# Routing as single operations behind every sixth product, small two-operand ones on GpSimd

## The chip, the core and the metric

One NeuronCore of a Trainium2 chip runs the kernel. The metric is device time in microseconds for one execution, the median of several; lower is better. The engines of the core work side by side, each through its own queue in order: TensorE (PE in the profile, PEld its weight loads), VectorE (DVE), ScalarE (ACT), GpSimd (POOL) and the queue that issues most DMAs (SP).

## What is computed

A linear attention with a feature map, and behind it a mixture of experts in which every token goes to one expert (top 1 of 8).

```python
def phi(x):
    proj = np.einsum('bhsd,df->bhsf', x, w_phi)
    proj = proj - np.max(np.abs(proj), axis=-1, keepdims=True)
    return np.concatenate([np.exp(proj), np.exp(-proj)], axis=-1)
q_p, k_p = phi(q), phi(k)
kv = np.einsum('bhsf,bhsd->bhfd', k_p, v)
z = np.sum(k_p, axis=2)
attn = np.einsum('bhsf,bhfd->bhsd', q_p, kv) / (np.einsum('bhsf,bhf->bhs', q_p, z)[..., None] + 1e-06)
x = attn.transpose(0, 2, 1, 3).reshape(N, D)        # N = 4608 tokens, D = 512

logits = x @ w_gate                                 # 8 experts
expert_idx = np.argmax(logits, axis=1)
probs = np.exp(logits - logits.max(-1, keepdims=True))
probs /= probs.sum(-1, keepdims=True) + 1e-09
gate_w = probs[np.arange(N), expert_idx]
for e in range(8):
    mask = expert_idx == e
    out[mask] = gate_w[mask, None] * (np.maximum(x[mask] @ w1[e], 0.0) @ w2[e])
```

There are 8 batches, 8 heads, 576 positions and 64 elements per head; the hidden size of an expert is 1024.

## The kernel before

**Attention.** The work is cut into 16 units: 4 groups of two batches (`NG`), and in each group 4 pairs of heads (`NPR`). A unit projects q and k (`project`, L246 to L253): three products into a PSUM tile `ps_proj`, of which there are two, then on VectorE a maximum `mx` (L252) and a difference `t` (L253). The difference ends the use of the PSUM tile, so that TensorE can begin the next projection but one only when `t` is done. ScalarE takes exponentials of `t` (for q after a transpose `pt` on TensorE, L284, which reads `t`). k's exponentials are split into two parts, `kh` on ScalarE and `kl` on GpSimd or VectorE (L275); the raw inputs are split likewise (`xh`, `xl`, L234 and L235) and so is v (`vh`, `vl`, L302 and L303). The products of k with v go to `pk` (L315), one `pk` for each batch. A copy `kvT` by ScalarE (L332) follows each. Four small products `pf` (L341) fold the gate's weights in, and the products `pn` (L363) of q's features give the attention output and the logits, which VectorE normalizes (`rec`, `xrow`, `lgc`).

**Order.** Python emits the unit's work as two lists of items which `merge` interleaves by their weights: the features of this and the next unit on one side, and `first_half` or `second_half`, the products of the previous unit, on the other. `ordered` ties the products into one sequence. The tile framework's scheduler may then move instructions by priority, which normally follows the emission order and which `tc.high_priority` raises. The result is a fixed queue for each engine.

**Routing.** When the four units of a group are through, the group's tokens are routed: `route` (from L571) sums the logits (`lg`), takes the maximum (`lmax`), subtracts it, marks the first expert that reaches it (`cand`, `choice`, `oh_b`), counts tokens of each expert (`gsum`, `base`), and finds each token's rank within its expert by ten bf16 products into `prk` with a triangle of ones. From the ranks come `rkb` (rank divided by 128) and `rkr` (its remainder) and for each of nine token tiles two selection matrices, `sel_p` on VectorE and `sel_h` on GpSimd. The gate value is computed from `ex` and `se` and stored (`gt`). `prk`, `pk` and `pf` share one PSUM pool of two buffers, `ps_kv`, so that the buffer of `prk` is free again only after the product `rks` (L631) has read it. The steps of `route` are a list of functions; `spread` puts one behind every eighth item of the half units of the next group, from its second unit on (u = 5, 9 and 13). For the last group the routing runs by itself, in two parts (`final` is False or True there and None before), between attention and experts. Before the last group's end, `lead` picks the fullest expert from the first three groups, so that its weights can be loaded early.

**Experts.** Tokens are gathered by expert into blocks of 128, 17 pairs of blocks and then single ones, and pass through two products split into three parts each (L936 to L938, L956 to L958).

## Time and profile before

| | |
|---|---|
| median of 3 runs | 953.48 us (951.97 to 954.35) |
| the profiled execution | 955.01 us, of which its span 953.2 us |
| mean granted TensorE clock | 0.968 of full speed |
| PE busy | 909.2 us, 95% |
| VectorE, ScalarE, GpSimd busy | 607.4, 592.6 and 489.3 us |

The span runs from the first to the last instruction. A row of the timeline gives start, duration, engine, line and operation, the tiles written and read, their shapes, how many instructions are merged in the row, and in brackets how long the engine had been idle and what released it. Attention fills the first 440 us or so, the experts the rest.

### The profile page before, as it was taken

The numbers are of one execution on the slowest core, as the hardware profiler recorded it, in microseconds if no ns is written. First come the engines' busy times: TensorE is split into PE (matmuls) and PEld (weight loads), VectorE is DVE, ScalarE is ACT, GpSimd is POOL, SyncE is SP. The second block draws the span as 40 slices with busy tenths as digits, with TensorE's granted clock in tenths as the row PEclk, the third lists the DMA queues.
The fourth block names the chain that finished last, engine by engine and source line by source line (L and its number), as shares of the span: only waits on it lengthen the run. The fifth ranks groups of instructions, "written<-read, shape, count | busy, mean of one in ns | idle before, by whom it ended". The sixth has DMA issues, their size and how long they took to land. (4 is left out here: it accounts for less than half of the span.)

```text
span 953.2 us, 18418 instructions
## 1 busy us (share of the span) xinstructions
PE 909.2 (95%) x6824; PEld 853.8 (90%) x6824; DVE 607.4 (64%) x1046; ACT 592.6 (62%) x895; POOL 489.3 (51%) x325
## 2 busy tenths in 40 slices
PE   6999989999899989999899999999999999999995
PEld 5899989999799989998889999999999999987884
DVE  7767778677987779865854444444444444457850
ACT  5977765777758765762565555555555555568961
POOL 6656666766476667653453333333333333347741
PEclk7999998999999998997999999999999999999998
DMA  4333332333233332143024224341343643764100
GB/s 146 90 103 102 97 100 78 89 107 92 60 103 103 104 102 68 48 147 118 17 95 156 67 91 154 127 150 56 105 155 113 211 154 122 225 219 136 44 23 14
DMA packets 64348, 102.38 MB, mean 107 GB/s; under 512 B 10686, under 2 KB 28478, under 8 KB 64256
## 3 DMA queue, kind: packets, MB, share of 16 engines
q1 hardware_dynamic: 56928, 80.34, 27.3%
q0 software_dynamic: 6720, 20.80, 7.0%
q8 instruction: 54, 0.88, 0.4%
q14 instruction: 38, 0.31, 0.1%
q10 hardware_dynamic: 608, 0.05, 0.0%
HBM read 136.74 MB, written 20.26 MB: 165 GB/s over the span
## 5 line engine op out<-in xcount | busy, mean ns | idle before, releaser
L894 DVE TENSOR_TENSOR wl<-raw,wh 128x1024 fp32r<-128x1024 f32 x137 | 181.2, 1336 | 139.3 <-ACT wh L893 135.4
L893 ACT CAST wh<-raw 128x1024 fp32r<-128x1024 f32 x184 | 191.6, 1050 | 102.7 <-PE po L958 69.2
L894 POOL TENSOR_TENSOR wl<-raw,wh 128x1024 fp32r<-128x1024 f32 x47 | 117.8, 2510 | 176.7 <-ACT wh L893 169.2
L363 PE MATMUL pn<-kf,qp 128*128 128x73 f32 x1024 | 160.9, 261 | 0.0
L363 PEld LDWEIGHTS pn<-kf,qp 128*128 128x128 f32 x1024 | 155.6, 198 | 0.2
L937 PE MATMUL pm<-xl,wh 128*128 128x256 f32 x544 | 154.8, 285 | 0.0
L938 PE MATMUL pm<-xh,wl 128*128 128x256 f32 x544 | 154.7, 284 | 0.0
L936 PE MATMUL pm<-xh,wh 128*128 128x256 f32 x544 | 154.2, 284 | 0.0
L252 DVE TENSOR_REDUCE mx<-ps_proj 128x4 f32<-128x512 f32 (+1 forms) x160 | 100.7, 631 | 70.5 <-PE ps_proj L248 70.2
L275 POOL TENSOR_TENSOR kl<-e,kh 128x1024 fp32r<-128x1024 f32 x47 | 112.9, 2402 | 57.5 <-ACT kh L273 57.5
L235 POOL TENSOR_TENSOR xl<-xr,xh 128x512 fp32r<-128x512 f32 (+2 forms) x62 | 87.0, 1406 | 92.0 <-ACT xh L234 92.0
L246 PE MATMUL ps_proj<-w_hi,xh 128*128 128x256 f32 x288 | 93.8, 326 | 16.8 <-DVE choice L589 10.0
L956 PE MATMUL po<-wh,hh 128*128 128x512 f32 x272 | 109.6, 403 | 0.0
L957 PE MATMUL po<-wl,hh 128*128 128x512 f32 x272 | 107.4, 395 | 0.0
L958 PE MATMUL po<-wh,hl 128*128 128x512 f32 x272 | 106.8, 392 | 0.7 <-DVE hl L944 0.7
L937 PEld LDWEIGHTS pm<-xl,wh 128*128 128x128 f32 x544 | 105.0, 193 | 2.5
L936 PEld LDWEIGHTS pm<-xh,wh 128*128 128x128 f32 x544 | 104.8, 193 | 2.6
L938 PEld LDWEIGHTS pm<-xh,wl 128*128 128x128 f32 x544 | 105.0, 193 | 0.0
L253 DVE TENSOR_TENSOR t<-ps_proj,mx 128x512 f32<-128x512 f32 (+1 forms) x160 | 100.9, 632 | 3.2
L315 PE MATMUL pk<-kh,vl 128*64 128x256 f32 x320 | 99.0, 309 | 2.4 <-POOL vl L303 2.4
L315 PE MATMUL pk<-kl,vh 128*65 128x256 f32 x320 | 99.6, 311 | 1.2 <-POOL kl L275 0.8
L315 PE MATMUL pk<-kh,vh 128*65 128x256 f32 x320 | 99.6, 311 | 0.3 <-DVE vh L302 0.3
(207 smaller groups left out, 2048.8 us busy)
## 6 DMA issues: line engine op xcount, KB each, us to landing
raw<-w SPq DMA_DIRECT2D x184, 512.0 KB
vt<-vv SPq DMA_DIRECT2D x16, 640.0 KB
x_dram<-xrow SPq DMA_DIRECT2D x30, 256.0 KB
xr<-kT SPq DMA_DIRECT2D x15, 320.0 KB
xr<-qT SPq DMA_DIRECT2D x15, 320.0 KB
xr<-kT SPq DMA_DIRECT2D x17, 256.0 KB
xr<-qT SPq DMA_DIRECT2D x17, 256.0 KB
x_dram<-xrow SPq DMA_DIRECT2D x32, 32.0 KB
```

Of the source, the lines that this page charges most:

```text
L253: V.tensor_tensor(t[:, 0 : 2 * n, :], psv, mx[:, 0 : 2 * n].unsqueeze(2).to_broadcast([P, 2 * n, F]), op=ALU.subtract,)
L275: eng.tensor_tensor(kl, e[:, 0:m], kh, op=ALU.subtract)
L315: return T.matmul(st["pk", bb][0:n, hh, :], (vl if j == 1 else vh)[:, 2 * (c + (bb if c == 8 else 0)) + hh, 0:n], (kl if j == 2 else kh)[: ...
L363: m = T.matmul(st["pn"][:, 2 * (c % 3) + hh, :], qp[:, s, s0 + hh, :] if c < 8 else qp[:, s, hh, bb : bb + 2].rearrange("p b q -> p (b q)" ...
L893: A.copy(th, raw[k])
L894: (G if k in (POOL_LO if u else POOL_LO0) else V).tensor_tensor(tl, raw[k], th, op=ALU.subtract)
L936: T.matmul(pm[:, i], th, xh[:, k, :], start=(k == 0), stop=False)
L937: T.matmul(pm[:, i], th, xl[:, k, :], start=False, stop=False)
L938: T.matmul(pm[:, i], tl, xh[:, k, :], start=False, stop=(k == KD - 1))
L956: T.matmul(po, hh[:, i, r], th[:, c], start=(i == j == 0), stop=False)
L957: T.matmul(po, hh[:, i, r], tl[:, c], start=False, stop=False)
L958: T.matmul(po, hl[:, i, r], th[:, c], start=False, stop=(i == 1 and j == 3))
```

## The change

The functions of `route` become one operation each for the three early routings, and `spread` puts one behind every sixth item. The variable `X` stands for VectorE in the last group's routing and for GpSimd in the three others; on `X` run the subtraction of the maximum, the two operations of `cand`, the copies `onehot`, `base_b`, `blk`, `rkr` and `gt`, and the additions to `base` and `se`. Reductions, `oh_b`, the two integer operations on the ranks, the reciprocal and `sel_p` stay on VectorE. The product `rks` is emitted right behind the matmuls of `prk`, for the early routings at a raised priority. For the last group the functions are joined again into steps like those of before. Line numbers of the new code lie up to 34 further down.

```diff
--- before.py
+++ after.py
@@ -458,7 +458,7 @@
         res, k = [], 0
         for i, it in enumerate(items):
             res.append(it)
-            if i >= 8 and i % 8 == 0 and k < len(steps):
+            if i >= 6 and i % 6 == 0 and k < len(steps):
                 res.append((0, steps[k]))
                 k += 1
         del steps[:k]
@@ -574,45 +574,61 @@
         js = slice(j0, j0 + n)
         r = {}
 
-        def choose():
-            lg = sg.tile([P, NC, E], F32, name="lg")[:, 0:n]
+
+
+        X = V if final is not None else G
+
+        def tile_of(name, shape, dtype=F32, **kw):
+            r[name] = sg.tile(shape, dtype, name=name, **kw)[:, 0:n]
+            return r[name]
+
+        def logits():
             V.tensor_reduce(
-                lg, lgc[:, c0 : c0 + n].rearrange("p c h e -> p c e h"), axis=AX.X, op=ALU.add
+                tile_of("lg", [P, NC, E]),
+                lgc[:, c0 : c0 + n].rearrange("p c h e -> p c e h"),
+                axis=AX.X,
+                op=ALU.add,
             )
-            lmax = sg.tile([P, NC], F32, name="lmax")[:, 0:n]
-            V.tensor_reduce(lmax, lg, axis=AX.X, op=ALU.max)
-            V.tensor_tensor(lg, lg, lmax.unsqueeze(2).to_broadcast([P, n, E]), op=ALU.subtract)
-            cand = sg.tile([P, NC, E], F32, name="cand")[:, 0:n]
-            V.tensor_scalar(cand, lg, 0.0, -float(E), op0=ALU.is_ge, op1=ALU.mult)
-            V.tensor_tensor(cand, cand, iota_e.unsqueeze(1).to_broadcast([P, n, E]), op=ALU.add)
-            first = choice[:, js]
-            V.tensor_reduce(first, cand, axis=AX.X, op=ALU.min)
-            oh_b = sg.tile([P, NC, E], BF16, name="oh_b")[:, 0:n]
+
+        def top():
+            V.tensor_reduce(tile_of("lmax", [P, NC]), r["lg"], axis=AX.X, op=ALU.max)
+
+        def shift():
+            X.tensor_tensor(r["lg"], r["lg"], r["lmax"].unsqueeze(2).to_broadcast([P, n, E]), op=ALU.subtract)
+
+        def candidates():
+            cand = tile_of("cand", [P, NC, E])
+            X.tensor_scalar(cand, r["lg"], 0.0, -float(E), op0=ALU.is_ge, op1=ALU.mult)
+            X.tensor_tensor(cand, cand, iota_e.unsqueeze(1).to_broadcast([P, n, E]), op=ALU.add)
+
+        def first_top():
+            V.tensor_reduce(choice[:, js], r["cand"], axis=AX.X, op=ALU.min)
+
+        def one_hot():
+            oh_b = tile_of("oh_b", [P, NC, E], BF16)
             V.tensor_tensor(
                 oh_b,
                 iota_em.unsqueeze(1).to_broadcast([P, n, E]),
-                first.unsqueeze(2).to_broadcast([P, n, E]),
+                choice[:, js].unsqueeze(2).to_broadcast([P, n, E]),
                 op=ALU.is_equal,
             )
-            r["lg"], r["oh_b"] = lg, oh_b
+            X.tensor_copy(onehot[:, js, :], oh_b)
+            r["base_b"] = sg.tile([P, E], BF16, name="base_b")
+            X.tensor_copy(r["base_b"], base)
 
         def count():
-            oh_b = r["oh_b"]
-            oh = onehot[:, js, :]
-            base_b = sg.tile([P, E], BF16, name="base_b")
-            V.tensor_copy(base_b, base)
             if final:
                 pc = ps_kv.tile([P, E], F32, name="pc", tag="pk")
-                T.matmul(pc, ones, base_b, start=True, stop=False)
+                T.matmul(pc, ones, r["base_b"], start=True, stop=False)
                 for c in range(n):
-                    T.matmul(pc, ones, oh_b[:, c, :], start=False, stop=(c == n - 1))
+                    T.matmul(pc, ones, r["oh_b"][:, c, :], start=False, stop=(c == n - 1))
                 place(pc)
-            V.tensor_copy(oh, oh_b)
+
+        def sum_up():
             if not final:
                 gsum = sg.tile([P, E], F32, name="gsum")
-                V.tensor_reduce(gsum, oh.rearrange("p c e -> p e c"), axis=AX.X, op=ALU.add)
-                V.tensor_tensor(base, base, gsum, op=ALU.add)
-            r["base_b"] = base_b
+                V.tensor_reduce(gsum, onehot[:, js, :].rearrange("p c e -> p e c"), axis=AX.X, op=ALU.add)
+                X.tensor_tensor(base, base, gsum, op=ALU.add)
 
         def count_ranks():
             oh_b, base_b = r["oh_b"], r["base_b"]
@@ -624,21 +640,21 @@
                     prk[:, c + 1 :, :], ones, oh_b[:, c : c + 1, :].to_broadcast([P, m, E]), start=False, stop=False
                 )
             T.matmul(prk, ones, base_b.unsqueeze(1).to_broadcast([P, n, E]), start=False, stop=True)
-            r["prk"] = prk
+            with tc.high_priority(offset=200 if final is None else 0):
+                V.tensor_tensor(tile_of("rks", [P, NC, E]), prk, onehot[:, js, :], op=ALU.mult)
 
         def rank():
-            rks = sg.tile([P, NC, E], F32, name="rks")[:, 0:n]
-            V.tensor_tensor(rks, r["prk"], onehot[:, js, :], op=ALU.mult)
-            rki = sg.tile([P, NC], I32, name="rki")[:, 0:n]
             with nc.allow_low_precision("ranks are integers"):
-                V.tensor_reduce(rki, rks, axis=AX.X, op=ALU.add)
-            rkb = sg.tile([P, NC], I32, name="rkb")[:, 0:n]
-            V.tensor_single_scalar(rkb, rki, 7, op=ALU.arith_shift_right)
-            V.tensor_copy(blk[:, js], rkb)
-            V.tensor_single_scalar(rki, rki, P - 1, op=ALU.bitwise_and)
-            rkr = sg.tile([P, NC], F32, name="rkr", bufs=2)[:, 0:n]
-            V.tensor_copy(rkr, rki)
-            r["rkr"] = rkr
+                V.tensor_reduce(tile_of("rki", [P, NC], I32), r["rks"], axis=AX.X, op=ALU.add)
+
+        def rank_parts():
+            rkb = tile_of("rkb", [P, NC], I32)
+            V.tensor_single_scalar(rkb, r["rki"], 7, op=ALU.arith_shift_right)
+            V.tensor_single_scalar(r["rki"], r["rki"], P - 1, op=ALU.bitwise_and)
+
+        def rank_values():
+            X.tensor_copy(blk[:, js], r["rkb"])
+            X.tensor_copy(tile_of("rkr", [P, NC], bufs=2), r["rki"])
 
         def select_a(c):
 
@@ -657,18 +673,36 @@
                 )
 
         def gate():
-            ex = sg.tile([P, NC, E], F32, name="ex")[:, 0:n]
-            A.activation(ex, r["lg"], AF.Exp)
-            se = sg.tile([P, NC], F32, name="se")[:, 0:n]
-            V.tensor_reduce(se, ex, axis=AX.X, op=ALU.add)
-            V.tensor_scalar_add(se, se, 1e-9)
-            V.reciprocal(se, se)
+            A.activation(tile_of("ex", [P, NC, E]), r["lg"], AF.Exp)
+
+        def gate_sum():
+            V.tensor_reduce(tile_of("se", [P, NC]), r["ex"], axis=AX.X, op=ALU.add)
+            X.tensor_scalar_add(r["se"], r["se"], 1e-9)
+
+        def gate_store():
+            V.reciprocal(r["se"], r["se"])
             gt = sg.tile([P, NC, XW - DM], F32, name="gt", bufs=2)
-            V.tensor_copy(gt[:, 0:n], se.unsqueeze(2).to_broadcast([P, n, XW - DM]))
+            X.tensor_copy(gt[:, 0:n], r["se"].unsqueeze(2).to_broadcast([P, n, XW - DM]))
             store_rows(g, gt, DM, XW - DM, c0, n)
 
-        steps = [choose, count, count_ranks, rank] + [lambda c=c: select(c) for c in range(n)] + [gate]
-        return steps if final is not None else [choose] + PAUSE * [pause] + steps[1:3] + PAUSE * [pause] + steps[3:]
+        steps = [logits, top, shift, candidates, first_top, one_hot]
+        selects = [lambda c=c: select(c) for c in range(n)]
+        ranks = [rank, rank_parts, rank_values]
+        gates = [gate, gate_sum, gate_store]
+        if final is not None:
+
+            def all_of(fs):
+                return lambda: run(fs)
+
+            return [
+                all_of(steps),
+                all_of([count, sum_up]),
+                count_ranks,
+                all_of(ranks),
+                *selects,
+                all_of(gates),
+            ]
+        return steps + [sum_up] + PAUSE * [pause] + [count_ranks, pause] + ranks + selects + gates
 
 
     ON_ACT = (0, 2, 4, 6, 8)
```

**VectorE at the beginning of an early routing, before.** `lg` to `oh_b` are the routing's, `mx` and `t` the projections'.

```order
L584 TENSOR_TENSOR lg<-lg,lmax 128x72
L252 TENSOR_REDUCE mx<-ps_proj 128x4
L586 TENSOR_SCALAR cand<-lg 128x72
L663 TENSOR_REDUCE se<-ex 128x9
L587 TENSOR_TENSOR cand<-cand,iota_p 128x72
L253 TENSOR_TENSOR t<-ps_proj,mx 128x512
L589 TENSOR_REDUCE choice<-cand 128x9
L252 TENSOR_REDUCE mx<-ps_proj 128x4
L591 TENSOR_TENSOR oh_b<-iota_em,choice 128x72
L253 TENSOR_TENSOR t<-ps_proj,mx 128x512
```

VectorE at the same place after the change, from `lmax` on:

```order
L594 TENSOR_REDUCE lmax<-lg 128x9
L253 TENSOR_TENSOR t<-ps_proj,mx 128x512
L252 TENSOR_REDUCE mx<-ps_proj 128x4
L605 TENSOR_REDUCE choice<-cand 128x9
L253 TENSOR_TENSOR t<-ps_proj,mx 128x512
L609 TENSOR_TENSOR oh_b<-iota_em,choice 128x72
L252 TENSOR_REDUCE mx<-ps_proj 128x4
L630 TENSOR_REDUCE gsum<-onehot 128x8
L253 TENSOR_TENSOR t<-ps_proj,mx 128x512
```

Three of the routing's operations went to GpSimd, the sum `se` stands further down, and `choice` and `gsum` now stand where a result of GpSimd is waited for, with a `t` behind each.

**GpSimd at the same place after the change.** Before, only `kl` and `xl` stood here.

```order
L275 TENSOR_TENSOR kl<-e,kh 128x1024
L597 TENSOR_TENSOR lg<-lg,lmax 128x72
L601 TENSOR_SCALAR cand<-lg 128x72
L235 TENSOR_TENSOR xl<-xr,xh 128x512
L602 TENSOR_TENSOR cand<-cand,iota_p 128x72
L275 TENSOR_TENSOR kl<-e,kh 128x1024
L615 CAST onehot<-oh_b 128x72
```

The moved operations stand between the splits of k and of the inputs: the second operation of `cand` behind an `xl`, `onehot` behind a `kl`.

**VectorE in the second half of an early routing, before.** `kf` is the copy of the four `pf`.

```order
L351 COPY kf<-pf 128x292
L636 TENSOR_SCALAR rkb<-rki 128x9
L253 TENSOR_TENSOR t<-ps_proj,mx 128x256
L637 CAST blk<-rkb 128x9
L638 TENSOR_SCALAR rki<-rki 128x9
L664 TENSOR_SCALAR se<-se 128x9
L603 CAST base_b<-base 128x8
L640 CAST rkr<-rki 128x9
L665 RECIPROCAL se<-se 128x9
L655 TENSOR_SCALAR sel_p<-iota_pb,rkr,part_133 128x128 x6
```

Between `kf` and the first `sel_p` stand eight operations, of which seven are the routing's. VectorE there after the change, from the `t` behind `kf` on:

```order
L253 TENSOR_TENSOR t<-ps_proj,mx 128x512
L644 TENSOR_TENSOR rks<-prk,onehot 128x72
L648 TENSOR_REDUCE rki<-rks 128x9
L252 TENSOR_REDUCE mx<-ps_proj 128x4
L652 TENSOR_SCALAR rkb<-rki 128x9
L253 TENSOR_TENSOR t<-ps_proj,mx 128x512
L390 TENSOR_SCALAR rec<-pn 128x6
L653 TENSOR_SCALAR rki<-rki 128x9
L391 RECIPROCAL rec<-rec 128x6
L393 TENSOR_TENSOR xrow<-pn,rec 128x384
L399 TENSOR_TENSOR lgc<-pn,rec 128x3x16
L671 TENSOR_SCALAR sel_p<-iota_pb,rkr,part_133 128x128 x9
```

`rks` stands behind the copy `kf` and no longer ahead of it, the casts and the `se` operations are gone, and the nine `sel_p` now stand in one row.

**GpSimd at that second place, after the change.** `blk` and `rkr` were VectorE's before.

```order
L303 TENSOR_TENSOR vl_158<-vt,vh_156 128x1280
L617 CAST base_b<-base 128x8
L656 CAST blk<-rkb 128x9
L235 TENSOR_TENSOR xl<-xr,xh 128x512
L657 CAST rkr<-rki 128x9
L671 TENSOR_SCALAR sel_h<-iota_pb,rkr,hbase 128x128 x4
L275 TENSOR_TENSOR kl<-e,kh 128x1024
L671 TENSOR_SCALAR sel_h<-iota_pb,rkr,hbase 128x128 x5
```

`rkr`, which `sel_p` and `sel_h` read, stands behind a `vl` and an `xl`.

## Rows read from the trace of the kernel before

**Rows 1.** Waits of PE: line waited for and releaser, us in total, times, longest.

```profile
PE ps_proj L246 <- DVE choice L589: 10.0, 3, 3.4
...
PE pf L341 <- DVE rks L631: 3.9, 3, 1.3
PE pp L834 <- DVE bsel L823: 2.5, 1, 2.5
```

**Rows 2.** Timeline of ACT: the copy `kvT` that ends a unit (columns as above).

```profile
129.92 0.58 ACT L332 COPY kvT<-pk 65x512 f32<-65x512 f32 x1 [2.75 <-PE pk L315]
...
164.33 0.58 ACT L332 COPY kvT<-pk 65x512 f32<-65x512 f32 x1 [3.00 <-PE pk L315]
...
188.63 0.58 ACT L332 COPY kvT<-pk 65x512 f32<-65x512 f32 x1 [1.82 <-PE pk L315]
...
237.30 0.58 ACT L332 COPY kvT<-pk 65x512 f32<-65x512 f32 x1 [2.75 <-PE pk L315]
...
270.38 0.58 ACT L332 COPY kvT<-pk 65x512 f32<-65x512 f32 x1 [2.98 <-PE pk L315]
...
343.38 0.58 ACT L332 COPY kvT<-pk 65x512 f32<-65x512 f32 x1 [2.76 <-PE pk L315]
...
376.49 0.58 ACT L332 COPY kvT<-pk 65x512 f32<-65x512 f32 x1 [2.99 <-PE pk L315]
```

**Rows 3.** Timeline of PE at the stops of the first routing and at one of `lead`.

```profile
137.64 0.36 PE L246 MATMUL ps_proj<-w_hi,xh 128*128 128x256 f32 x1
...
142.64 0.55 PE L246 MATMUL ps_proj<-w_hi,xh 128*128 128x256 f32 x1 [3.34 <-DVE choice L589]
...
154.34 0.44 PE L341 MATMUL pf<-fold,kvT 65*128 65x73 f32 x2 [1.29 <-DVE rks L631]
...
403.65 0.39 PE L246 MATMUL ps_proj<-w_hi,xh 128*128 128x256 f32 x1 [1.29 <-DVE t L253]
```

**Rows 4.** Stretches of 5 us: length, busy (x instructions) of PE, PEld, DVE, ACT, POOL; PEclk.

```profile
140.00:145.00 5.00, 2.36 (x12) 2.39 (x13) 4.66 (x9) 2.19 (x3) 1.81 (x2) 0.71 0.21 59
...
405.00:410.00 5.00, 4.84 (x52) 4.84 (x53) 4.65 (x9) 3.03 (x7) 0.40 (x1) 1.00 0.24 69
```

**Rows 5.** Timeline of DVE at the beginning of the first routing.

```profile
136.09 0.21 DVE L583 TENSOR_REDUCE lmax<-lg 128x9 f32<-128x72 f32 x1
...
138.61 1.76 DVE L586 TENSOR_SCALAR cand<-lg 128x72 f32<-128x72 f32 x1
...
140.43 1.47 DVE L587 TENSOR_TENSOR cand<-cand,iota_p 128x72 f32<-128x72 f32 x1
141.82 0.68 DVE L253 TENSOR_TENSOR t<-ps_proj,mx 128x512 f32<-128x512 f32 x1
...
143.15 0.22 DVE L591 TENSOR_TENSOR oh_b<-iota_em,choice 128x72 bf16<-128x72 f32 x1
```

**Rows 6.** Timeline of POOL in the first routing.

```profile
136.71 1.28 POOL L235 TENSOR_TENSOR xl<-xr,xh 128x512 fp32r<-128x512 f32 x1 [6.18 <-ACT xh L234]
137.95 2.37 POOL L275 TENSOR_TENSOR kl<-e,kh 128x1024 fp32r<-128x1024 f32 x1
...
154.97 2.68 POOL L303 TENSOR_TENSOR vl<-vt,vh 128x1280 fp32r<-128x1280 f32 x1
```

**Rows 7.** Groups of POOL instructions by line: count, busy us, mean ns, idle before.

```profile
L154 POOL TENSOR_SCALAR neg_h<-hbase 128x36 f32<-128x36 f32 x1 | 1.1, 1065 | 0.1
...
L844 POOL TENSOR_TENSOR ends<-start,singles 1x8 f32<-1x8 f32 x1 | 0.2, 191 | 1.1 <-DVE start L563 1.1
```

**Rows 8.** Timeline of DVE in the second half of the first routing.

```profile
156.08 1.60 DVE L636 TENSOR_SCALAR rkb<-rki 128x9 int32<-128x9 int32 x1
...
159.25 1.51 DVE L655 TENSOR_SCALAR sel_p<-iota_pb,rkr,part 128x128 bf16<-128x128 bf16 x6
...
165.13 0.42 DVE L252 TENSOR_REDUCE mx<-ps_proj 128x2 f32<-128x256 f32 x1
```

**Rows 9.** Timeline of POOL in a unit without routing.

```profile
195.41 1.30 POOL L235 TENSOR_TENSOR xl<-xr,xh 128x512 fp32r<-128x512 f32 x1 [5.36 <-ACT xh L234]
```

## The prediction

> **What bounds the kernel now.** Read first who makes TensorE wait, since it is busy nearly all the time. Of the waits that fall into attention, the largest is that of a projection for VectorE's `choice`, 10.0 us in 3 times, and another is that of `pf` for `rks`, 3.9 us in 3 times [rows 1]: one of each for each early routing, 13.9 us together.
>
> Then read what a unit takes, from the copy `kvT` at its end to the next one. The unit behind the first routing takes 188.63 - 164.33 = 24.30 us. The three units in which a routing begins take 34.41, 33.08 and 33.11 us [rows 2]. Against 24.30 that is 10.11, 8.78 and 8.81, in all **27.7 us**. So 13.8 us more are lost than the stops show. The reader sees where at the first routing: TensorE stops 3.34 us and 1.29 us [rows 3], and in the slice around the first stop the granted clock is 0.71, a mixture of the full 2.4 GHz and of half of it [rows 4]. I read the 13.8 us as work at the lower level behind six stops, 2.3 us for each (the ranks' own short products are in it). Not every stop is followed by it: the one of 1.29 us at 403.65 [rows 3] has a clock of 1.00 in the slice behind it [rows 4].
>
> Last, why VectorE is late. `cand` has 72 elements in a row of the tile and yet took 1.76 us, its second operation 1.47 us, while `lmax`, which reads as many, took 0.21 us [rows 5]. The 1.76 us end at 140.37, and GpSimd's `kl`, 2.37 us long, ends at 140.32 [rows 6]. Operations on VectorE without a reduction, with all operands in SBUF, stand still here while GpSimd works on a large two-operand one. Behind them stands `t`, 141.82 to 142.50, and TensorE goes on at 142.64.
>
> **The change part by part.**
>
> *The moved operations at the first stop.* Off VectorE's path go the subtraction and both of `cand`. They now run on GpSimd, and `choice` waits for them there. I replay the first routing. `lmax` ends at 136.30 [rows 5]. The price of a small operation on GpSimd does not show in this form; the nearest rows are 0.19 us for 8 elements of two operands and 1.07 us for 36 elements of one [rows 7]. I take 0.3 us, near the lower row, because that one has two operands and waited for nobody, and from the large ones: `kl` takes 2.37 us for 1024 elements, so 72 are 0.17 us plus a start. Then: subtraction to 136.6, first `cand` to 136.9, the `xl` in between (1.28 us [rows 6]) to 138.2, second `cand` to 138.5, `choice` to 138.7, `t` (0.68) to 139.4. TensorE stopped 3.34 us before 142.64, at 139.3. With the handing over it stops about 0.3 us instead of 3.3.
>
> *What is late next.* `oh_b` stays on VectorE behind that `t`, and its operands are all in SBUF. In its row it took 0.22 us [rows 5], but GpSimd was between two of its large operations then. After the change a `kl` starts at 138.5 and holds until 140.9. I take it that `oh_b` waits as `cand` did, to 141.0; `mx` behind it to 141.6; `onehot` on GpSimd meanwhile to 141.3; `gsum` to 141.8; the next `t` to 142.5. TensorE needs that `t` for a transpose. What it has before that is six projection products and four others; the same kind of run went from 137.64 to 139.3 before the stop [rows 3], 1.6 us with the drain. So from 139.6 it works to 141.0 or a little later and then stops 1.5 us. Together the first place costs 1.8 us of stop instead of 3.3.
>
> The Trainium skill, page "SBUF — State Buffer", section "Who interferes with whom", says that a VectorE operation with two SBUF inputs contends with a GpSimd one that reads SBUF, that the loser blocks for the whole instruction, and that a reduction never contends. The trace agrees in the 1.76 and the 0.21 us of [rows 5]; by that rule the stop behind `oh_b` stands, by `oh_b`'s own row of 0.22 us it would not.
>
> *Ranks right behind their matmuls.* `rks` is no longer queued behind other work with the pool's buffer in its hand, and the `prk` products now stand behind the four `pf` of their half unit, not ahead of them. The 1.29 us stop of `pf` goes, three times. What hides the next wait for that buffer is the rest of the half unit's products.
>
> *Ranks to selections.* Before, from the first `sel_p` at 159.25 to the next `mx` at 165.13, VectorE served no projection for 5.9 us and TensorE did not stop [rows 8]: that long its other products cover. In the new order there is no projection served from the `t` behind `rkb` through all nine `sel_p`. Between them: the integer remainder, which may stand still for a `vl` of 2.68 us [rows 6], as `rkb` did for 1.60 us [rows 8], I take 2.2; `rec`, `xrow` and `lgc`, some 0.9; the wait for `rkr`, which GpSimd does behind `blk` and an `xl`, 0.3 + 1.28 + 0.3 less the 0.9 = 1.0; nine `sel_p` at 1.51 / 6 [rows 8] = 2.3. The sum is 6.4, from 4.2 without the `vl` to 6.9 with all of it. Over the cover of 5.9 it is 0 to 1.0, and as TensorE now runs at the full clock there, where cover is used up fastest, I take 1.0, the upper end.
>
> *The rest, at nothing.* The gate's operations moved to GpSimd are not waited for by TensorE; they run in GpSimd's gaps, 5.36 us at once in a unit without routing [rows 9], and would cost their 0.3 us each if the gaps were gone. One step behind six products and not behind eight makes 27 steps fit in one and a half units as 20 did. The last group's routing keeps its operations on VectorE; only their order changes a little ahead of `bsel`, for which TensorE waits 2.5 us [rows 1]; between half a microsecond gained and lost, I take 0. DMA queues get the same transfers; the store of `gt` on SP now waits for GpSimd, with the next input loads behind it, and comes earlier in the routing than before, so I count nothing.
>
> **Sum.** Stops for one routing: 1.8 + 1.0 = 2.8 us instead of 4.6. Of the lower clock: the stop of 1.5 us is longer than all that were followed by it (1.29), that of 1.0 us is shorter, so I count the first always and the second in half of the cases: 4.5 times 2.3 = 10.4 us for three routings. Left of the 27.7 us are 3 x 2.8 + 10.4 = 18.8 us, and the gain is 8.9 us. I take 1 us off, for stops of some tenths that the new handings between engines bring, and forecast a gain of **8 us**. The profiled execution would go from 955.0 (span 953.2) to 947.0. It stands 1.5 us above the median of 953.5; by that the median goes to **945.5 us**.
>
> **Rivals.**
>
> *The waits only change their place.* If the small operations cost what the dearer row says, 1.07 us [rows 7], three of them and `onehot` are 3.1 us later than in the replay; the first stop is then 2.6 us or more, the second as before, all six stops are followed by the lower clock, and 3 x (2.6 + 1.5 + 1.0) + 13.8 = 29 us stand against 27.7: 953.5 to 955, no difference. For it speaks that GpSimd does them in order between operations of 1.28 to 2.68 us. Against it speaks the row of 0.19 us.
>
> The Trainium skill, page "Perfetto Trace Analysis", section "Optimizing Scalar/DVE Operations", warns that moving work from VectorE to GpSimd might not help, because they share a read port; by it this rival is the forecast. The trace shows the sharing, but also that the moved operations pay it now.
>
> *`oh_b` does not wait.* Its only rows are short. Then the stop of 1.5 us is gone, and left are 3 x (0.3 + 1.0) and three times 2.3 us at most, 10.8 us: a gain of 17, 936.5.
>
> *Slower: GpSimd's queue holds up the products.* `gt` on GpSimd waits for VectorE's reciprocal, and other small ones for `lmax`, `oh_b`, `gsum` and `se`; behind each stand the `kl`, `xl` and `vl` that the products of k and v need. It decides when these waits and the ten operations (3 us) together are more than the 5.36 us of idle time [rows 9]. If three of the waits are as long as a `kl`, 7.1 us, 4.7 us come through in each routing, on top of the 2.8, with at least two spells of the lower clock: 3 x (4.7 + 2.8 + 4.6) = 36.3 against 27.7, 8.6 us slower, 962.
>
> **Chances.** Forecast (a gain of 3 to 12 us) 0.60, `oh_b` free 0.14, only a change of place 0.19, held-up products 0.07. A difference of 0.3%, 2.9 us, is about what a measurement can tell from none. Faster by more: 0.74, within: 0.19, slower: 0.07. The range leaves out the slower rival and the better part of the `oh_b` one and reaches into the no-difference case: 939 to 952.5.
>
> **What would show it.** In the new profile: the wait for `choice` at 0.5 us or less in the three places and none of `pf` for `rks` (right); `oh_b` at 1 us or more in the mean, and a transpose `pt` or a projection waiting 1 to 2 us for VectorE just after; a projection waiting some 1 us behind the nine `sel_p`; units of 28 to 32 us in which a routing begins, and perhaps the next one a little long. Wrong would be: `kl` of GpSimd as a new releaser of `pk`, small operations of 1 us on GpSimd, or an `oh_b` of 0.2 us.

## The result and the profile after

The changed kernel takes **942.32 us** (median; 937.23 to 942.77) against 953.06 us beside it: ratio 0.9866, 95% interval 0.9846 to 0.9886. Run a second time, beside the last experiments, it took 938.97 us against 954.45, ratio 0.9845 (0.9821 to 0.9869). By the medians it is faster by 10.7 us in the first comparison and by 15.5 in the second, where 8 were forecast; the ratios on record are not the quotients of these medians, which are 0.9887 and 0.9838. The profiled execution went from 955.0 to 942.1 us. All of its 12.9 us lie in attention: at the first `kvT` of [rows 2] the two traces agree (129.92 and 129.87 us), and the last `kvT` stands at 434.28 us before and at 421.39 after.

Waits of TensorE after the change (line waited for and releaser, us in total, times, longest), to be read against [rows 1]:

```profile
PE pt L284 <- DVE t L253: 9.2, 7, 1.6
...
PE ps_proj L246 <- DVE t L253: 3.1, 5, 0.8
```

No wait of TensorE is put down to `choice` or `rks` any more. In their place stand short ones for `t`, most often of the transposes. The copies `kvT` on ScalarE, which answer [rows 2]:

```profile
129.87 0.58 ACT L332 COPY kvT<-pk 65x512 f32<-65x512 f32 x1 [2.75 <-PE pk L315]
...
158.76 0.58 ACT L332 COPY kvT<-pk 65x512 f32<-65x512 f32 x1 [2.64 <-PE pk L315]
...
183.15 0.58 ACT L332 COPY kvT<-pk 65x512 f32<-65x512 f32 x1 [2.76 <-PE pk L315]
...
231.81 0.58 ACT L332 COPY kvT<-pk 65x512 f32<-65x512 f32 x1 [2.75 <-PE pk L315]
...
262.12 0.58 ACT L332 COPY kvT<-pk 65x512 f32<-65x512 f32 x1 [2.65 <-PE pk L315]
...
335.16 0.58 ACT L332 COPY kvT<-pk 65x512 f32<-65x512 f32 x1 [2.76 <-PE pk L315]
...
364.11 0.58 ACT L332 COPY kvT<-pk 65x512 f32<-65x512 f32 x1 [2.66 <-PE pk L315]
```

The three units with a routing take 28.89, 30.31 and 28.95 us instead of 34.41, 33.08 and 33.11; the unit behind the first takes 24.39. The excess of the three over 24.30 us fell from 27.7 to 15.3 us. TensorE's stops at the first routing [rows 3]:

```profile
139.86 0.36 PE L246 MATMUL ps_proj<-w_hi,xh 128*128 128x256 f32 x1 [0.61 <-DVE t L253]
...
142.82 0.63 PE L284 MATMUL pt<-ident,t 128*128 128x128 f32 x4 [1.43 <-DVE t L253]
...
154.34 0.66 PE L284 MATMUL pt<-ident,t 128*128 128x128 f32 x4 [1.55 <-DVE t L253]
```

Three stops, 3.6 us together, where there were two of 4.6. The second and third routing show the same three within 0.04 us. Stretches of 5 us around stops (length, busy of PE, PEld, DVE, ACT, POOL, then PEclk, DMA share and GB/s), as [rows 4]:

```profile
140.00:145.00 5.00, 3.57 (x32) 3.40 (x33) 5.00 (x8) 3.98 (x8) 4.20 (x5) 1.00 0.16 47
...
245.00:250.00 5.00, 5.00 (x35) 5.00 (x35) 4.45 (x12) 3.26 (x6) 2.31 (x3) 0.72 0.23 54
...
360.00:365.00 5.00, 5.00 (x51) 5.00 (x49) 4.62 (x18) 1.97 (x5) 4.79 (x7) 1.00 0.87 250
```

Between 120 and 395 us the granted clock fell at one place only, around 245 us; behind the other stops it stayed at 1.00. Before, it fell around all three first stops [rows 4] and behind all three second ones, of which the first is:

```profile
155.00:160.00 5.00, 5.00 (x36) 5.00 (x35) 4.64 (x15) 2.66 (x5) 4.57 (x4) 0.66 0.48 128
```

Summing (1 - PEclk) times 5 us over the stretches from 120 to 395 us gives 11.9 us before and 1.7 after. That, and not the stops (13.9 and 10.7 us), is where most of the gain of this pair of profiles lies. There is one profile of the kernel before, and its mean granted clock of 0.968 is at the low end of that kernel's executions (0.968 to 0.984), so its 11.9 us may be more than usual.

VectorE at the two places:

```profile
138.89 0.23 DVE L605 TENSOR_REDUCE choice<-cand 128x9 f32<-128x72 f32 x1 [1.46 <-POOL cand L602]
139.03 0.68 DVE L253 TENSOR_TENSOR t<-ps_proj,mx 128x512 f32<-128x512 f32 x1
139.63 1.66 DVE L609 TENSOR_TENSOR oh_b<-iota_em,choice 128x72 bf16<-128x72 f32 x1
...
142.00 0.67 DVE L253 TENSOR_TENSOR t<-ps_proj,mx 128x512 f32<-128x512 f32 x1
...
151.34 2.35 DVE L652 TENSOR_SCALAR rkb<-rki 128x9 int32<-128x9 int32 x1
153.61 0.68 DVE L253 TENSOR_TENSOR t<-ps_proj,mx 128x512 f32<-128x512 f32 x1
...
155.92 2.30 DVE L671 TENSOR_SCALAR sel_p<-iota_pb,rkr,part 128x128 bf16<-128x128 bf16 x9
```

And GpSimd:

```profile
136.32 0.31 POOL L597 TENSOR_TENSOR lg<-lg,lmax 128x72 f32<-128x72 f32 x1 [5.84 <-DVE lmax L594]
136.72 0.47 POOL L601 TENSOR_SCALAR cand<-lg 128x72 f32<-128x72 f32 x1
137.27 1.29 POOL L235 TENSOR_TENSOR xl<-xr,xh 128x512 fp32r<-128x512 f32 x1
138.51 0.34 POOL L602 TENSOR_TENSOR cand<-cand,iota_p 128x72 f32<-128x72 f32 x1
138.81 2.38 POOL L275 TENSOR_TENSOR kl<-e,kh 128x1024 fp32r<-128x1024 f32 x1
...
150.98 2.68 POOL L303 TENSOR_TENSOR vl<-vt,vh 128x1280 fp32r<-128x1280 f32 x1
...
155.27 0.19 POOL L657 CAST rkr<-rki 128x9 f32<-128x9 int32 x1
```

`oh_b` starts 0.8 us into `kl` and ends 0.1 us behind it; `rkb` starts 0.4 us into `vl` and ends 0.03 us behind it. Each time a `t` that TensorE needs stands behind it in VectorE's queue: at once behind `rkb`, and behind two short operations after `oh_b`.

### The profile page after: what moved, and what is told of

Same layout as the page of the kernel before. It is cut to its first block, busy times and chain, and to the rows that moved or that the text cites. A ratio compares the mean times of both kernels' runs of the same rounds, so it can differ in the third digit from the quotient of the medians.

```text
span 940.1 us, 18395 instructions
## 1 busy us (share of the span) xinstructions
PE 900.6 (96%) x6824; PEld 844.2 (90%) x6824; DVE 591.0 (63%) x1016; ACT 591.9 (63%) x895; POOL 499.4 (53%) x355
## 5 line engine op out<-in xcount | busy, mean ns | idle before, releaser
L928 DVE TENSOR_TENSOR wl<-raw,wh 128x1024 fp32r<-128x1024 f32 x137 | 183.6, 1353 | 139.2 <-ACT wh L927 135.7
L363 PE MATMUL pn<-kf,qp 128*128 128x73 f32 x1024 | 157.2, 256 | 0.0
L363 PEld LDWEIGHTS pn<-kf,qp 128*128 128x128 f32 x1024 | 151.2, 193 | 0.2
```

What stands on the lines that cost most here:

```text
L363: m = T.matmul(st["pn"][:, 2 * (c % 3) + hh, :], qp[:, s, s0 + hh, :] if c < 8 else qp[:, s, hh, bb : bb + 2].rearrange("p b q -> p (b q)" ...
L928: (G if k in (POOL_LO if u else POOL_LO0) else V).tensor_tensor(tl, raw[k], th, op=ALU.subtract)
```

## The experiments

Every variant computes the whole kernel, except where that is said. Each diff is against the changed kernel. Ratios are against the kernel before, run on the same chip. The runs are numbered in the order in which they were made, which is not that of the text. Runs 1 to 4 and 9 to 12 were on one chip, runs 5 to 8 on another.

**The three parts, one by one.** First all the two-operand operations back on VectorE:

```diff
-        X = V if final is not None else G
+        X = V
```

> The changed kernel, but the small operations of the early routings on VectorE again; single steps, spacing of six and the early rank product stay. Theory A (TensorE stops because a routing operation on VectorE stands still for a large GpSimd one with the next difference t queued behind it): the subtraction and the two operations of cand take 1.2 to 1.8 us each again, the first projection stop is 2 to 3 us again, and the time goes back to 949 to 955. Theory B (what helped is that the routing is cut into single steps with products between them): 940 to 944, and the small operations find gaps.

Measured in run 1: 942.84 us, ratio 0.9895 (0.985 to 0.994). TensorE's first stop is 1.95 us, close to theory A's 2 to 3, but the time is theory B's. So at this spacing most of the gain is there without the move to GpSimd, on which the prediction had rested it. The ranks' product back in its old place:

```diff
-            with tc.high_priority(offset=200 if final is None else 0):
-                V.tensor_tensor(tile_of("rks", [P, NC, E]), prk, onehot[:, js, :], op=ALU.mult)
+            r["prk"] = prk
...
         def rank():
+            V.tensor_tensor(tile_of("rks", [P, NC, E]), r["prk"], onehot[:, js, :], op=ALU.mult)
```

> The changed kernel, but the rank product rks is emitted with the rank steps as before, without raised priority. Theory A: no one waits for its PSUM buffer any more because the ten rank products now stand behind the four pf of their half unit; 940 to 945, no wait of pf for rks. Rival: the early product is what removed the 1.29 us stop of pf; then it is back in three places, with the lower clock behind it, 946 to 953.

Measured in run 2: 941.91 us, 0.9866 (0.9841 to 0.9892), the same stops, and no wait of `pf` for `rks`. The early product itself gives nothing. That the stop left because the `prk` products now stand behind the `pf`, as theory A has it, is read from the queue and not shown: in run 4 below they stand ahead of the `pf` again (143.22 and 145.09 us), with the late product, and that wait does not come back either. The spacing of before:

```diff
-            if i >= 6 and i % 6 == 0 and k < len(steps):
+            if i >= 8 and i % 8 == 0 and k < len(steps):
```

> The changed kernel, but one step behind every eighth item. Theory A: the first two stops (0.6 and 1.4 us) stay, since the same operations meet the same kl; the ranks' steps meet other large GpSimd operations in the next unit, with one or two stops of 1 to 2.5 us; 943 to 950. Theory B: the spacing is a main part of the gain, 949 to 954.

Measured in run 3: 943.5 us, 0.988 (0.9849 to 0.991), the lower edge of theory A and not to be told from the changed kernel. And the move to GpSimd alone, with the steps joined as before, spacing eight and the late product:

```diff
+        def together(fs):
+            return lambda: run(fs)
...
-        return steps + [sum_up] + PAUSE * [pause] + [count_ranks, pause] + ranks + selects + gates
+            [together(steps)] + PAUSE * [pause] + [sum_up, count_ranks] + PAUSE * [pause]
+            + [together(ranks)] + selects + [together(gates)]
```

> Only the move to GpSimd: steps in the coarse groups of before with the pauses of before, one behind every eighth item, rank product with the ranks. Theory A: the first stop is 0.6 and 1.4 us as in the changed kernel instead of 3.3; the integer operations on the ranks still wait for vl or xl, up to 3 us in one place; 943 to 950. Theory B: coarse groups stop TensorE as before, 951 to 955.

Measured in run 4: 950.46 us, 0.9966 (0.9948 to 0.9984). GpSimd alone is worth some 3 us, its time between those of the two theories; the first two stops are theory A's (0.6 and 1.4 us), and one of 2.4 to 2.6 us is added at the ranks. So the steps as single operations looked like the whole change, and they were tried without the rest, with the diffs of runs 1 to 3 together (VectorE, late product, every eighth):

> One part of the change alone: the routing of the middle chunks in single operations, with the spacing of before (one behind every eighth product), the product of the ranks where it stood before, and all the two-operand arithmetic on VectorE. Theory S (the single steps are the change; spacing, early product and GpSimd are small additions to it): as the run with VectorE alone, 940 to 947 us, ratio 0.987 to 0.993 against before, since in that run only spacing and the early product were left beside the single steps, and each of them measured as nothing. Theory T (the parts need each other: at one operation behind every eighth product the routing lasts longer and meets the large GpSimd operations of another place): 949 to 955 us. What decides in the trace: under S a subtraction t of the projection stands between the two operations on the candidates, and the stops in front of ps_proj and pt together take 11 to 14 us.

Measured in run 5: 949.53 us, 0.9958 (0.9944 to 0.9972). Theory S fell and T holds: no `t` stands between the two operations on the candidates, and the stops take 15.5 us. The single steps alone bring 4 us, though taking away any one of the other parts had cost 3 us at most. To find which pair does it, and to rule out the chip, the changed kernel was run again, unaltered, beside the variants between runs 1 and 5.

> The changed kernel itself, unaltered, on the chip of the next three runs, so that the variants that differ in one part can be set against it. In the first set of experiments a variant with the whole routing on VectorE took 942.8 us, in the second set one that differs from it only in spacing and in the place of the ranks' product took 949.5 us, on another chip. Theory U (that difference lies in the kernels): the changed kernel repeats its 942 us here, 940 to 944, ratio 0.986 to 0.989. Theory W (it lies in the chip: the clock falls behind more of the same stops on some chips): 945 to 950 us here.

Measured in run 9: 938.97 us, 0.9845 (0.9821 to 0.9869). This is again the chip of runs 1 to 4, so the repetition alone does not decide between U and W; run 11 does. Beside it the kernel of run 1, with the diff on `X` alone:

> The changed kernel with the small two-operand operations on VectorE (spacing of six, early ranks' product), a second time. Theory U: 941 to 944 us, as the first time, and within 2 us of the changed kernel beside it: GpSimd gives nothing where the spacing is six. Theory V (its first measurement of four executions, 940.3 to 948.5 us, was a lucky one; the move to GpSimd is worth several us beside the single steps): 946 to 950 us, over 4 us above the changed kernel beside it. By the stops alone (12.8 us in its profile against 11.4 of the changed kernel) it should be 1 to 2 us slower.

Measured in run 10: 942.96 us, 0.9887 (0.9868 to 0.9907). Theory V's 946 and more is excluded; theory U's 2 us of distance was too small, since the changed kernel beside it is 4.0 us faster (the two intervals only touch). Then the diff on `X` and that on the spacing together:

> The same with one operation behind every eighth product, the early product of the ranks kept: one step between the run with VectorE alone and the run with single steps alone. If spacing is the difference between those two: 948 to 951 us, with the stop of 2.7 us before pt (the second operation on the candidates directly before a t) that the run with single steps alone showed at all three places. If the early product is the difference: 941 to 945 us and no such stop.

Measured in run 11: 949.44 us, 0.9948 (0.9934 to 0.9961), on the chip on which run 10 took 942.96. So the kernels differ, not the chips. And the diff on `X` and that on the ranks' product together:

> The same with one operation behind every sixth product and the ranks' product where it stood before: the other step between the two runs. If spacing is the difference: within 2 us of the run with VectorE alone beside it, stops of 1.95, 0.3 and 1.9 us as in that run. If the early product is the difference: 948 to 951 us.

Measured in run 12: 941.39 us, 0.9867 (0.9849 to 0.9885). So **spacing** is the difference, and the early product is none, twice over. Ratios with single steps:

| small operations on | one behind every eighth | behind every sixth |
|---|---|---|
| VectorE | 0.9948; 0.9958 (late product) | 0.9895, 0.9887; 0.9867 (late product) |
| GpSimd | 0.988 | 0.9866, 0.9845; 0.9866 (late product) |

By these ratios 4 to 5 us are gained with spacing eight on VectorE. The finer spacing or GpSimd, either one, brings it to 10 to 13 us, and both to 13 to 15 us. Runs 5 and 11 agree on two chips. Why is read from VectorE in run 11 (spacing eight, VectorE):

```profile
136.50 1.79 DVE L601 TENSOR_SCALAR cand<-lg 128x72 f32<-128x72 f32 x1
138.21 0.68 DVE L252 TENSOR_REDUCE mx<-ps_proj 128x4 f32<-128x512 f32 x1
138.81 1.50 DVE L602 TENSOR_TENSOR cand<-cand,iota_p 128x72 f32<-128x72 f32 x1
140.23 0.68 DVE L253 TENSOR_TENSOR t<-ps_proj,mx 128x512 f32<-128x512 f32 x1
```

its TensorE, and its clock there:

```profile
141.05 1.08 PE L284 MATMUL pt<-ident,t 128*128 128x128 f32 x4 [2.69 <-DVE t L253]
```

```profile
140.00:145.00 5.00, 3.95 (x24) 3.98 (x24) 4.41 (x11) 2.12 (x4) 0.21 (x1) 0.66 0.19 56
```

and from VectorE and TensorE in run 10 (spacing six, VectorE):

```profile
138.56 1.77 DVE L601 TENSOR_SCALAR cand<-lg 128x72 f32<-128x72 f32 x1
...
140.40 0.68 DVE L253 TENSOR_TENSOR t<-ps_proj,mx 128x512 f32<-128x512 f32 x1
140.99 0.88 DVE L602 TENSOR_TENSOR cand<-cand,iota_p 128x72 f32<-128x72 f32 x1
```

```profile
141.22 0.36 PE L246 MATMUL ps_proj<-w_hi,xh 128*128 128x256 f32 x1 [1.96 <-DVE t L253]
```

In both, the first operation of `cand` stands still beside `kl` and the second beside an `xl`, as before the change. With spacing eight both are ahead of the next `t`; with six a `t` comes in between. On GpSimd they take 0.47 and 0.34 us, and only `choice` waits for them. Each is another way of having no `t` behind two stalled operations.

**What the remaining stops hang on.** Theory P: the shared access of VectorE and GpSimd to SBUF makes `oh_b` and `rkb` long, and without that the stops go. Theory Q: any operation that waits will do, for SBUF or for a result of GpSimd, if a `t` stands behind it. First `oh_b` moved to GpSimd:

```diff
+                G.tensor_tensor(
+                    far,
+                    iota_em.unsqueeze(1).to_broadcast([P, n, E]),
+                    choice[:, js].unsqueeze(2).to_broadcast([P, n, E]),
+                    op=ALU.subtract,
+                )
+                G.tensor_scalar(oh_b, far, 0.0, 1.0, op0=ALU.is_equal, op1=ALU.mult)
```

> The changed kernel with one operation moved: the one-hot comparison of the middle chunks (1.66 us on VectorE, where it stood still beside kl on GpSimd, with t behind it) is done on GpSimd, as a subtraction and a comparison behind kl; the sum of the one-hots stays on VectorE. Theory P (the stop of 1.43 us before pt is the price of the two-input operation on VectorE that has to share with GpSimd): the stop is gone or under 0.5 us at all three places, 936 to 940 us. Theory Q (any VectorE operation of the routing that depends on GpSimd holds the t queued behind it; which one is not important): the stop stays at 1 to 2.2 us, now behind the operation that sums the one-hots, which waits for GpSimd; 940 to 945 us.

Measured in run 6: 950.08 us, 0.9953 (0.9934 to 0.9972), above what either theory gave. The changed kernel itself was not run on the chip of these three runs; that the chip makes no such difference is argued from runs 5 and 11 alone. VectorE and TensorE:

```profile
139.04 0.28 DVE L640 TENSOR_REDUCE gsum<-onehot 128x8 f32<-128x72 f32 x1 [2.26 <-POOL onehot L625]
139.24 0.68 DVE L253 TENSOR_TENSOR t<-ps_proj,mx 128x512 f32<-128x512 f32 x1
```

```profile
140.07 1.09 PE L284 MATMUL pt<-ident,t 128*128 128x128 f32 x4 [2.35 <-DVE t L253]
```

Q holds as a mechanism: nothing contends, `gsum` waits for GpSimd, and the stop is longer than the one it replaces (1.43 us). Its time was missed because the clock fell behind all three of these stops. Next, the division of the ranks moved to GpSimd; this version does not compute the kernel's ranks, so it is read for its stops alone:

```diff
+                G.tensor_scalar(blk[:, js], r["lmax"], 1.0 / P, 0.5 / P - 0.5, op0=ALU.mult, op1=ALU.add)
+                G.tensor_scalar(blk[:, js], blk[:, js], 8388608.0, -8388608.0, op0=ALU.add, op1=ALU.add)
...
+                G.tensor_scalar(rkr, blk[:, js], -float(P), 0.0, op0=ALU.mult, op1=ALU.add)
+                G.tensor_tensor(rkr, rkr, r["lmax"], op=ALU.add)
```

> The changed kernel with the division of the ranks moved: block and remainder of the rank are computed on GpSimd in floating point (rounding by adding and taking away 2 to the 23rd) instead of by the integer shift rkb (2.35 us on VectorE beside vl on GpSimd) and the integer mask. Theory P: the stop of 1.5 us before pt behind rkb is gone or under 0.5 us; 936 to 940 us. Theory Q: VectorE now waits with the nine sel_p, or another operation that needs the remainder, until GpSimd has finished vl and the four small operations behind it, with a t behind: a stop of 1.5 to 3.5 us; 941 to 947 us.

Measured in run 7: 951.62 us, 0.9981 (0.9965 to 0.9996). VectorE and TensorE:

```profile
153.74 0.32 DVE L683 TENSOR_SCALAR sel_p<-iota_pb,rkr,part 128x128 bf16<-128x128 bf16 x1 [3.65 <-POOL rkr L666]
153.97 0.68 DVE L253 TENSOR_TENSOR t<-ps_proj,mx 128x512 f32<-128x512 f32 x1
```

```profile
154.71 0.65 PE L284 MATMUL pt<-ident,t 128*128 128x128 f32 x4 [3.08 <-DVE t L253]
```

The same again: the stop of 1.55 us has become one of 3.08, behind the first `sel_p`, as Q had it; the time is above Q's 941 to 947 us. Last, a version meant to be faster. It holds `choice` and the gate's sum and reciprocal behind the `t` written last before them, makes `oh_b` on GpSimd as in run 6, sums the one-hots there too, and adds pauses; of its diff are shown the first hold and the pauses:

```diff
+            behind_t(V.tensor_reduce(choice[:, js], r["cand"], axis=AX.X, op=ALU.min), final is None)
...
+            steps[:4] + 2 * [pause] + steps[4:] + 0 * [pause] + [sum_up] + PAUSE * [pause]
+            + [count_ranks, pause] + ranks + 2 * [pause] + selects + 0 * [pause] + gates
```

> A version meant to beat the changed kernel: the operation that finds the first maximum and the sum of the gates are held behind the t written last before them, so that a t never queues behind an operation of the routing that waits; the one-hots are summed on GpSimd by additions, and the steps lie two groups of products further apart at two points. Theory Q: the two stops at the first place (0.61 and 1.43 us) shrink to one of under 1 us at each of three places; what remains is the ranks' place, where the nine sel_p come later, with a stop of 2 to 4.5 us before ps_proj: 936 to 944 us, centre 941. If the stops only gather at the ranks' place and the clock falls behind them: 944 to 950 us.

Measured in run 8: 946.0 us, 0.9928 (0.9905 to 0.9951): the second of the two cases in the expectation, and slower than the changed kernel was on the other chip. VectorE, TensorE and the clock at the ranks' place:

```profile
156.19 1.29 DVE L699 TENSOR_SCALAR sel_p<-iota_pb,rkr,part 128x128 bf16<-128x128 bf16 x5 [4.78 <-POOL rkr L685]
157.40 0.41 DVE L254 TENSOR_REDUCE mx<-ps_proj 128x2 f32<-128x256 f32 x1
```

```profile
158.42 0.58 PE L248 MATMUL ps_proj<-w_hi,xh 128*128 128x256 f32 x1 [3.81 <-DVE t L255]
```

```profile
155.00:160.00 5.00, 1.58 (x7) 1.58 (x8) 3.81 (x16) 1.35 (x3) 4.89 (x8) 0.79 0.35 121
160.00:165.00 5.00, 5.00 (x28) 5.00 (x27) 3.68 (x7) 1.81 (x4) 3.55 (x5) 0.53 0.22 66
```

The first place has no stop left at all. But `sel_p` now waits 4.78 us for `rkr`, which stands behind an `xl` and a `kl` on GpSimd, and the next projection with it. Twelve us of stops, 10.9 of them in three long pieces, cost more than 10.7 in nine short ones.

**Stops and clock together**, from one profile each: the stops between 120 and 385 us, what the clock took from 120 to 395 us, summed as above, and the time from the `kvT` at some 128 us to the last one:

| kernel | profiled us | stops | longest | clock | `kvT` to last `kvT` |
|---|---|---|---|---|---|
| before | 955.0 | 13.9 | 3.35 | 11.9 | 304.4 |
| changed; again; late product | 942.1; 938.8; 942.2 | 10.7; 10.8; 10.8 | 1.56 | 1.7; 0.0; 1.7 | 291.5; 290.2; 291.6 |
| VectorE; again; late product | 942.5; 942.1; 940.9 | 12.1; 11.8; 12.5 | 1.96 | 3.5; 1.7; 0.0 | 294.5; 293.0; 292.2 |
| GpSimd, every eighth | 947.1 | 12.8 | 1.43 | 6.8 | 298.6 |
| GpSimd, joined steps | 944.7 | 14.7 | 2.61 | 3.5 | 297.7 |
| VectorE, every eighth, early; late product | 949.0; 948.8 | 14.9; 15.5 | 2.73 | 6.8; 3.4 | 301.1; 298.4 |
| `oh_b` on GpSimd | 945.7 | 12.8 | 2.35 | 8.5 | 299.1 |
| division on GpSimd | 952.2 | 17.1 | 3.08 | 8.5 | 304.6 |
| held behind `t` | 944.8 | 12.0 | 3.84 | 8.6 | 297.3 |

Taking stops and clock from the last column leaves 278.5 to 279.7 us in twelve of the fourteen traces, so within about 1 us the two are all that sets these kernels apart there. It leaves 277.8 and 276.7 us for `oh_b` on GpSimd and the version held behind `t`, where the clock is already low in the last microsecond or so of some of the stops, in which TensorE has nothing to lose.

One spell of the lower clock takes about 1.7 us in this sum (0.66 in one stretch of 5 us, as in run 11). Its price in time can be read ahead of all routing, where all these kernels do the same. At 43 to 46 us every trace has the same stop of 1.3 us; here the changed kernel and its repetition, with the stretch around it:

```profile
45.30 0.44 PE L341 MATMUL pf<-fold,kvT 65*128 65x73 f32 x2 [1.27 <-ACT kvT L332]
...
45.24 0.44 PE L341 MATMUL pf<-fold,kvT 65*128 65x73 f32 x2 [1.26 <-ACT kvT L332]
```

```profile
45.00:50.00 5.00, 4.71 (x29) 4.71 (x30) 2.45 (x5) 4.72 (x8) 3.73 (x2) 0.66 0.12 44
...
45.00:50.00 5.00, 4.76 (x45) 4.76 (x46) 3.42 (x7) 5.00 (x9) 3.79 (x2) 1.00 0.09 30
```

Five of the fourteen traces have the lower clock there, nine do not, and from the `kvT` ahead of it to the next takes 12.2 us in the five and 10.6 in the nine: 1.6 us for a spell. One more or less in an execution is 0.2%. The profile of joined steps is the fastest of ten executions, that of `oh_b` among the faster of seven, that of GpSimd with every eighth the slowest of four.

Of the 23 stops over 2 us in all these traces 20 have the lower clock around or right behind them; of the 51 between 1.2 and 2 us in the changed kernel and its variants, 8; but of the three of 1.29 us in the kernel before, all three. Shorter ones are not free of it: two of the three of 1.1 us in run 3 have it. What sets these apart is not shown by any run; the stop at 45 us shows that the length alone does not decide.

## Why the prediction was right, and where it was not

**The gain** was forecast as 8 us and came as 10.7, the profiled one as 12.9. That it came this close is in part luck: the clock term was too large by 8.7 us, and more stops and other losses took 5.2 of that back.

**First place: right.** The replay gave `choice` at 138.7, a first stop of 0.3 us and one of 1.5 us behind an `oh_b` held by `kl` until 141.0. The trace has `choice` ending at 139.12, 0.61 and 1.43 us, and `oh_b` ending at 141.29. The price of 0.3 us for a small operation on GpSimd held for two operands (0.31 and 0.34 us), and 0.47 for the first `cand`.

**Second place: a stop there, but a longer one and for another cause.** The step "Ranks to selections" put a stop of 1.0 us behind a remainder held by `vl` and nine `sel_p`. The nine `sel_p` cost 2.30 us as worked out, but no projection stops for them. What waits for `vl` is the operation ahead of the remainder, `rkb`, 2.35 us, and the stop of 1.55 us is that of a transpose behind it. `rkb`'s own row of 1.60 us stood in [rows 8] and was read only as a hint for the other operation. `pf` no longer waits, as forecast; but the first of the two reasons given, the early product, does nothing, since runs 2 and 12 lose nothing without it, and the other, the place of `prk` behind the `pf`, is not shown to be needed.

**The clock: mis-sized.** This is the term that failed. The sum counted 3 x 2.8 = 8.4 us of stops (measured 10.7) and 10.4 us of lower clock, 4.5 spells of 2.3 us. The trace has one spell and 1.7 us. Two things were wrong: that a stop of 1.5 us always brings it because those of 1.29 us had, and the price, since of the 13.8 us only 11.9 were clock, in some seven spells of 1.7 and not six of 2.3. Counted were 2.3 us too few of stops and 8.7 too many of clock; 2.9 us of the new excess (1.9 of the old) are neither, and the sum missed by 3.5 us, 15.3 left instead of 18.8.

**Spacing: wrong as a price of nothing.** With GpSimd it is worth 1 to 3 us, within the intervals; with VectorE 5 to 6 us (0.9948 against 0.9895 and 0.9887). It decides what stands between two `t`. The move to GpSimd, the step that the sum rested on, shortens the first place as forecast, but at spacing six the kernel without it is only 3 to 4 us slower by the ratios (0.9895 against 0.9866, 0.9887 against 0.9845), and with the late product no slower (0.9867 against 0.9866).

**Rivals.** "Only change their place" priced small operations on GpSimd at 1.07 us; rows of 0.19 to 0.47 us at both places exclude it; only the addition to `se`, which no `t` waits for, took 1.31 us, beside VectorE's own `kl`. "`oh_b` does not wait" is excluded by 1.66 us. "GpSimd's queue holds up the products" did not happen: no `pk` waits for `kl`, `xl` or `vl` in a routing unit. The warning of the Trainium skill, page "Perfetto Trace Analysis", section "Optimizing Scalar/DVE Operations", that a move from VectorE to GpSimd might not help, is nearly borne out for the move alone (0.9966, some 3 us) and not beside the single steps at spacing eight (0.9948 to 0.988). Of the Trainium skill, page "SBUF — State Buffer", the rule in section "Who interferes with whom" on two-input operations agrees with the trace: `oh_b` took 1.66 us beside `kl`, and 0.22 us in run 10, where GpSimd was idle. The two rows that the prediction named for it do not bear it out: the `cand` of 1.76 us reads one tensor and not two, and `lmax` with its 0.21 us ran ahead of the `xl` at 136.71, when GpSimd was idle [rows 6]. The rows that do are the second operation of `cand`, 1.47 us, and the reduction `se`, 0.22 us, both beside the same `xl` of the kernel before:

```profile
140.29 0.22 DVE L663 TENSOR_REDUCE se<-ex 128x9 f32<-128x72 f32 x1
...
140.27 1.53 POOL L235 TENSOR_TENSOR xl<-xr,xh 128x640 fp32r<-128x640 f32 x1
```

## What to carry to other kernels

Where a short side job shares an in-order engine with work that a busier engine needs, ask of each of its operations what it can wait for and what stands behind it; cut the job so that no needed operation stands behind two that can stall. Moving the operation to another engine removes the stall only if nothing that stays behind has to wait for its result: two of the moves tried here made the stop longer. Price long stops higher than their length, by what the clock did behind stops of that kernel, and take the count from several stops, not from the only two lengths at hand.

## What the runs showed of the hardware

Not expected: the same 1.4 to 1.6 us stops leave the granted clock alone in one execution and lower it once in the next (0.0 and 1.7 us for the changed kernel), and the same stop of 1.3 us at 45 us is followed by it in five of fourteen traces; so the scatter of some us between executions is partly a count of such spells. And an integer operation of nine elements with a constant (`rkb`) stands still beside GpSimd's `vl` for 2.35 us just as two-input ones do, while nine `sel_p` take 2.30 us in all beside GpSimd's `sel_h`, themselves no two-tensor operations. One `sel_p` of the kernel before took nearly as long as the nine, beside a `kl` (161.01 to 163.65 us):

```profile
161.45 2.25 DVE L655 TENSOR_SCALAR sel_p<-iota_pb,rkr,part 128x128 bf16<-128x128 bf16 x1
```

In the rows read here only the large two-operand operations of GpSimd held VectorE up.
